# Linear attention and SwiGLU in one kernel: zero matmuls in the awaited bank, a group in halves, and a new order

## The chip, the core and the metric

The kernel runs on one core of a Trainium2 chip. The metric is device time of one execution in microseconds (us). A core has engines that run their own instruction streams side by side: TensorE (PE in the profile, its weight loads PEld), VectorE (DVE), ScalarE (ACT), GpSimd (POOL) and SyncE (SP), which here only issues transfers. Each works through its instructions in order and waits on semaphores for the others. Matmuls write to PSUM, of which this kernel uses eight banks; transfers between memory and SBUF run on 16 DMA engines.

## The reference

Four sequences of 768 tokens, 8 heads of 48: a linear attention with a decay of its own for each channel (RWKV-6), and behind it a feed-forward block over the 3072 rows of 384.

```python
for t in range(S):
    cur = np.einsum('bhd,bhe->bhde', u[None] * kt, vt)
    y[:, :, t] = np.einsum('bhd,bhde->bhe', rt, state + cur)
    state = wt[:, :, :, None] * state + np.einsum('bhd,bhe->bhde', kt, vt)
...
rms = np.sqrt(np.mean(x * x, axis=-1, keepdims=True) + 1e-06)
xn = x / rms * rms_g
g = xn @ w_gate
silu = g * (1.0 / (1.0 + np.exp(-g)))
return (silu * (xn @ w_val) @ w_out)
```

Inputs and output are float32; `w_gate` and `w_val` are 384x1536, `w_out` is 1536x384.

## The kernel before, in words

The 768 tokens are cut into six chunks of 128, so there are 24 tiles (n, j): chunk n of sequence j. Each tile passes through small steps, each a function of (n, j):

- Loads on SP's queue: `load_r`, `load_k`, `load_v`, `load_w` (L246 to L270). Each of r, k and v has eight buffers; the ninth load waits until the first tile's are read. For chunks 0 and 1 w comes in one load.
- Decay: `ln` (ACT, L383), `cs_mm` (PE, L391: running sums by a triangular matrix, 384 columns, and eight matmuls of one column for the totals), `exp_r` and `exp_k` (ACT), then `r_mul`, `w_tot` (DVE) and `k_mul` (DVE, or POOL for the tiles in `K_POOL`), which write the scaled r and k. From chunk 2 on `cs_add` (DVE) makes the second sum.
- Transposes of scaled r and k: for chunks 0 and 1 `rk_pe` (PE, L470, eight matmuls into one bank) and `rk_tr` (L476), which copies the bank of 128x1024 two-byte values to SBUF, on ScalarE; later chunks use a DMA transpose on SP's queue.
- Scores: `q_mm` (PE, L485) into an even and an odd bank; `q_mask_e` (DVE) masks the even one; the odd one is either masked on VectorE (`ODD_DVE`) or copied by ScalarE (`q_copy_o`) and masked on POOL (`q_mask_o`).
- Bonus of the current token: `bonus_mul` (POOL, two products), `bonus_sum` (DVE), `bonus_v` (POOL). `cast_v` (POOL or, for `CAST_ACT`, ACT) makes v two bytes wide.
- Output and state: `y_mm` (PE, L532), `x_add` (DVE), `st_mm` (PE), `st_new` (DVE).
- Norm: `x_sq` (ACT), `x_rstd` (ACT or POOL), `xn_mul` (ACT); then for chunks 0 to 3 `xn_pe` (PE) and `xn_out` (DVE, times the gain), for chunks 4 and 5 a DMA transpose `xn_tr` and `xn_gain` (POOL).

The feed-forward part works on six groups of four tiles, 512 columns. For each of twelve slices f of 128 hidden units there are `gate_mm` and `val_mm` (three matmuls of 512 columns each, L600), `silu` (ACT) and `h_mul` (DVE). A gate and val pair is called two units here. Then come four `o_mm` of twelve matmuls of 384 columns (L630), `o_out` and `out_dma`; the last tile's output is cut in two halves of 192. Groups are not chunks: `COL` (L193) puts tiles (1,0) and (1,1) in group 0 and (0,2) and (0,3) in group 1, so group 0 is (0,0), (0,1), (1,0), (1,1), and the feed-forward part starts when these four have passed the norm. What comes before is called the head.

Weights come on POOL's queue and are made two bytes wide on the way: `load_gv` g.h (L348; g 0 is slices 0 to 3, g 1 slices 4 to 11; h 0 gate, 1 val) and `load_wo`.

PSUM banks stand in three rings (L220): a and b of two banks each, for sums, gate and val, and q of four for the rest. `psum` (L223) gives a step the bank of its ring that came free first.

The order of all steps is written out in `ORDER` (L25), and the engines' streams follow from it, as `manual_schedule` adds waits but moves nothing. It was found by annealing against a planner's costs. `warm` steps (L372) are zero matmuls of 384 columns into a bank of ring q that nothing reads: 15 stand in the head, 6 behind the last output matmul. Two small matmuls for u and the gain stand ahead of all steps (L332 to L337).

Of the kernel before, what the change touches and what calls it, by code (L numbers as in the profile page):

```python
# [30 lines left out]
bonus_v.0.0 load_w.0.3 q_mask_o.0.0 q_mm.1.0 k_mul.0.1 q_mask_o.1.0 cast_v.0.0 r_mul.1.1 rk_pe.0.1 y_mm.0.0 k_mul.1.1
load_r.0.2 warm.16.0 rk_pe.1.1 x_add.0.0 w_tot.0.1 st_mm.0.0 load_v.0.1 bonus_mul.0.1 load_gv.0.0 q_mask_e.1.0
rk_tr.0.1 bonus_sum.0.1 warm.14.0 ln.0.3 st_new.0.0 x_sq.0.0 load_v.1.1 q_mm.0.1 x_rstd.0.0 q_mask_e.0.1 y_mm.1.0
x_add.1.0 rk_tr.1.1 cast_v.1.1 cast_v.0.1 load_w.0.2 bonus_sum.1.1 xn_mul.0.0 bonus_v.0.1 load_k.0.3 load_r.0.3
cs_mm.0.3 bonus_v.1.1 q_mask_o.0.1 w_tot.1.1 st_mm.0.1 y_mm.0.1 x_add.0.1 x_sq.1.0 exp_r.0.3 ln.0.2 q_mm.1.1
load_k.0.2 st_mm.1.1 q_mask_e.1.1 cs_mm.0.2 st_new.0.1 q_mask_o.1.1 xn_pe.0.0 y_mm.1.1 load_gv.0.1 xn_out.0.0
load_gv.1.0 x_sq.0.1 exp_k.0.3 load_v.0.2 x_rstd.1.0 load_v.0.3 x_rstd.0.1 k_mul.0.3 xn_mul.0.1 exp_r.0.2 x_add.1.1
xn_pe.0.1 xn_mul.1.0 xn_pe.1.0 bonus_mul.0.3 load_k.1.2 warm.15.0 warm.10.0 xn_out.0.1 x_sq.1.1 xn_out.1.0 x_rstd.1.1
xn_mul.1.1 warm.6.0 r_mul.0.3 w_tot.0.3 warm.18.0 st_mm.1.0 xn_pe.1.1 rk_pe.0.3 xn_out.1.1 r_mul.0.2 load_r.1.2
w_tot.0.2 exp_k.0.2 gate_mm.0.0 val_mm.0.0 gate_mm.0.3 silu.0.0 load_gv.1.1 silu.0.3 h_mul.0.0 gate_mm.0.1 val_mm.0.3  # L40
gate_mm.0.2 bonus_sum.0.3 k_mul.0.2 silu.0.1 val_mm.0.1 gate_mm.0.9 rk_tr.0.3 h_mul.0.3 silu.0.2 silu.0.9 load_v.1.2
q_mm.0.3 load_k.1.3 st_new.1.1 val_mm.0.2 gate_mm.0.8 bonus_mul.0.2 q_copy_o.0.3 h_mul.0.1 gate_mm.0.5 rk_pe.0.2
h_mul.0.2 silu.0.8 rk_tr.0.2 st_new.1.0 gate_mm.0.6 val_mm.0.9 q_mm.0.2 load_r.1.3 silu.0.5 h_mul.0.9 val_mm.0.8
cast_v.0.2 q_mask_e.0.3 h_mul.0.8 cs_mm.1.2 q_copy_o.0.2 q_mask_o.0.3 load_v.1.3 bonus_sum.0.2 load_w.2.0 silu.0.6
exp_k.1.2 cast_v.0.3 st_mm.0.2 st_mm.0.3 y_mm.0.3 q_mask_o.0.2 load_w.2.1 bonus_v.0.2 st_new.0.3 cs_mm.1.3 exp_r.1.2
load_w.2.2 q_mask_e.0.2 load_r.2.0 val_mm.0.6 bonus_v.0.3 exp_k.1.3 exp_r.1.3 r_mul.1.2 load_wo.1.0 y_mm.0.2 k_mul.1.2
w_tot.1.2 val_mm.0.5 gate_mm.0.4 rk_pe.1.2 silu.0.4 h_mul.0.6 val_mm.0.4 st_new.0.2 h_mul.0.5 load_wo.0.0 rk_tr.1.2
gate_mm.0.11 silu.0.11 x_add.0.3 r_mul.1.3 q_mm.1.2 x_sq.0.3 q_copy_o.1.2 load_w.2.3 bonus_mul.1.2 load_wo.2.0
w_tot.1.3 k_mul.1.3 bonus_sum.1.2 val_mm.0.7 cast_v.1.2 h_mul.0.4 cast_v.1.3 q_mask_o.1.2 rk_pe.1.3 q_mask_e.1.2
rk_tr.1.3 gate_mm.0.7 gate_mm.0.10 silu.0.7 y_mm.1.2 q_mm.1.3 x_add.0.2 val_mm.0.11 h_mul.0.7 val_mm.0.10 x_sq.0.2  # L50
q_copy_o.1.3 x_rstd.0.3 bonus_v.1.2 x_add.1.2 h_mul.0.11 st_mm.1.3 xn_mul.0.3 silu.0.10 x_rstd.0.2 load_r.2.1
h_mul.0.10 bonus_mul.1.3 q_mask_o.1.3 ln.2.0 xn_pe.0.3 xn_out.0.3 q_mask_e.1.3 o_mm.0.0 y_mm.1.3 cs_mm.2.0
bonus_sum.1.3 x_sq.1.2 x_rstd.1.2 ln.2.1 o_out.0.0 load_k.2.0 cs_add.2.0 xn_mul.0.2 xn_mul.1.2 load_r.2.2 ln.2.2
o_mm.0.2 st_new.1.3 load_r.2.3 exp_r.2.0 xn_pe.0.2 load_k.2.1 load_k.2.2 bonus_v.1.3 x_add.1.3 x_sq.1.3 ln.2.3
cs_mm.2.1 cs_add.2.1 x_rstd.1.3 exp_r.2.1 o_out.0.2 xn_mul.1.3 load_k.2.3 xn_pe.1.2 o_mm.0.1 w_tot.2.0 r_mul.2.0
r_mul.2.1 bonus_mul.2.0 cs_mm.2.3 w_tot.2.1 exp_k.2.0 k_mul.2.0 cs_mm.2.2 xn_out.1.2 exp_k.2.1 k_mul.2.1 xn_pe.1.3
out_dma.0.0 bonus_mul.2.2 cs_add.2.2 exp_k.2.2 cs_add.2.3 exp_r.2.3 xn_out.1.3 o_mm.0.3 rk_tr.2.0 xn_out.0.2 rk_tr.2.1
exp_r.2.2 w_tot.2.2 r_mul.2.2 st_mm.1.2 val_mm.1.4 r_mul.2.3 gate_mm.1.6 w_tot.2.3 exp_k.2.3 o_out.0.3 gate_mm.1.4
silu.1.6 bonus_mul.2.3 k_mul.2.2 k_mul.2.3 val_mm.1.6 h_mul.1.6 silu.1.4 h_mul.1.4 gate_mm.1.7 gate_mm.1.10 st_new.1.2
load_v.2.1 bonus_sum.2.0 val_mm.1.10 load_v.2.0 silu.1.10 silu.1.7 bonus_mul.2.1 val_mm.1.7 gate_mm.1.5 o_out.0.1  # L60
# [628 lines left out]
```

## Time and profile before

| | |
|---|---|
| three runs | 205.40, 206.16 (median), 279.91 us |
| profiled execution | 206.26 us |
| its span, first to last instruction | 204.5 us |
| first gate matmul starts | 30.89 us |
| last output matmul starts its twelve | 200.38 us |
| DMA | 32.41 MB, mean 158 GB/s |

In rows of the timeline the first number is the start, the second the length until the last of the group has ended; matmuls overlap, so the distance between starts tells their pace. In a bracket stands how long the engine was idle ahead of the row and what it waited for. In rows of groups the busy time comes first, then the mean length of one in ns, then idle time. The granted clock is a share of TensorE's full clock.

### The profile page before, as it was taken

To read this page: it belongs to the slowest core of one execution; us is meant where nothing else is said; L and a number is where in the kernel's file an instruction comes from. 1 tells how busy PE (TensorE), PEld (TensorE's weight loads), DVE (VectorE), ACT (ScalarE), POOL (GpSimd) and SP (SyncE) were. 2 spreads that over 40 slices of the span, in tenths; PEclk is the share of its full clock that TensorE was granted. 3 is DMA by queue.
4 is the path that set the end of the run, shared out by engine and by line. 5 is a ranking of instruction groups with operands and counts; after the bars stand their busy time and mean duration, and the time that the engine had idled before them with its cause. 6 is when DMAs were issued, how large, how long until landed. Compare 5 with 4: busy or idle time off the path is not lost.

```text
span 204.5 us, 4369 instructions
## 1 busy us (share of the span) xinstructions
PE 191.3 (94%) x1553; PEld 113.5 (55%) x1573; DVE 151.7 (74%) x298; ACT 144.4 (71%) x287; POOL 126.6 (62%) x186
## 2 busy tenths in 40 slices
...
GB/s 148 239 222 229 196 179 205 191 194 194 188 187 170 185 186 197 214 192 212 208 160 219 227 208 160 213 189 114 69 196 125 90 23 20 77 0 74 83 58 98
DMA packets 121566, 32.41 MB, mean 158 GB/s; under 512 B 116420, under 2 KB 120392, under 8 KB 121544
## 3 DMA queue, kind: packets, MB, share of 16 engines
...
q14 instruction: 10, 0.08, 0.1%
...
## 4 chain that ended last, share of the span: by engine, by line
PE 69%; DMA 12%; POOL 8%; DVE 3%; issue 3%; ACT 2%; POOLq 1%; SPq 0%; DVEq 0%; ACTq 0%
PE ps_bu L602 10%; PE ps_av L602 9%; PE ps_au L602 9%; PE ps_bv L602 9%; PE ps_qz L634 5%; DMA wv_sb<-in_moe_w_val_dram 5%; PE ps_qx L634 4%; PE ps_qu L634 3%; DMA wo_sb<-in_moe_w_out_dram 3%; PE ps_qv L634 3%; DMA vt<-in_v_dram 2%; POOL ruk L458 2%; DMA rkT<-rk 1%; POOL ruk L457 1%; DMA xnt<-xn 1%
## 5 line engine op out<-in xcount | busy, mean ns | idle before, releaser
L620 DVE TENSOR_TENSOR ht<-ps_bu,sg 128x512 bf16<-128x512 f32 x38 | 26.1, 686 | 16.9 <-PE ps_bu L602 12.8
L634 PEld LDWEIGHTS <-ht 128*128 128x128 bf16 x300 | 28.3, 98 | 17.2 <-issue 0.4
L602 PEld LDWEIGHTS <-wg_sb 128*128 128x128 bf16 x216 | 23.7, 114 | 22.7 <-issue 2.3
L236 ACT ACTIVATE sg<-ps_av 128x512 bf16<-128x512 f32 x38 | 22.7, 597 | 14.0 <-PE ps_av L602 11.9
L602 PEld LDWEIGHTS <-wv_sb 128*128 128x128 bf16 x216 | 22.4, 115 | 17.9 <-DMA wv_sb<-in_moe_w_val_dram 0.4
L602 PE MATMUL ps_av<-xnt,wg_sb 128*128 128x512 bf16 x111 | 30.5, 379 | 0.4 <-DVE xnt L588 0.2
L602 PE MATMUL ps_bu<-xnt,wv_sb 128*128 128x512 bf16 x103 | 30.2, 381 | 0.6
L457 POOL TENSOR_TENSOR ruk<-rt,kt 128x384 f32<-128x384 f32 x24 | 24.7, 1028 | 9.2 <-DMA rt<-in_r_dram 8.7
L620 DVE TENSOR_TENSOR ht<-ps_bv,sg 128x512 bf16<-128x512 f32 x34 | 23.3, 686 | 8.5 <-PE ps_bv L602 5.2
L602 PE MATMUL ps_au<-xnt,wg_sb 128*128 128x512 bf16 x97 | 27.0, 380 | 1.2 <-POOL xnt L593 0.8
L236 ACT ACTIVATE sg<-ps_au 128x512 bf16<-128x512 f32 x34 | 20.3, 597 | 10.4 <-PE ps_au L602 8.3
L602 PE MATMUL ps_bv<-xnt,wv_sb 128*128 128x512 bf16 x101 | 27.6, 381 | 0.0
L458 POOL TENSOR_TENSOR ruk<-ruk,u_bc 128x384 f32<-128x384 f32 x24 | 24.6, 1024 | 1.9
L467 POOL TENSOR_TENSOR ydiag<-vt,diag 128x384 f32<-128x384 f32 x24 | 19.8, 831 | 5.7 <-DVE diag L462 5.7
L234 ACT ACT_TABLE_LOAD x16 | 20.5, 1283 | 1.9 <-PEq L673 1.6
L510 POOL TENSOR_SCALAR_AFFINE_SELECT qts<-qts 128x512 bf16<-128x512 bf16 x20 | 12.6, 638 | 13.3 <-ACT qts L503 13.3
L634 PE MATMUL ps_qz<-wo_sb,ht 128*128 128x384 bf16 x96 | 17.1, 326 | 0.2 <-DMA wo_sb<-in_moe_w_out_dram 0.2
L563 ACT ACTIVATE xn<-xb,rstd 128x384 bf16<-128x384 f32 x24 | 14.3, 606 | 3.8 <-POOL rstd L559 3.6
L550 ACT ACTIVATE junk<-xb 128x384 bf16<-128x384 f32 x24 | 12.4, 518 | 6.0 <-DVE xb L545 5.5
L634 PE MATMUL ps_qx<-wo_sb,ht 128*128 128x384 bf16 (+1 forms) x84 | 13.8, 315 | 0.0
L462 DVE TENSOR_REDUCE diag<-ruk 128x8 f32<-128x384 f32 x24 | 12.8, 542 | 0.5 <-POOL ruk L458 0.5
L236 ACT ACTIVATE lw<-wt 128x384 bf16<-128x384 f32 (+1 forms) x20 | 11.4, 579 | 1.5 <-DMA wt<-in_w_dram 1.4
...
## 6 DMA issues: line engine op xcount, KB each, us to landing
...
wg_sb<-in_moe_w_gate_dram POOLq DMA_DIRECT2D x1, 768.0 KB, 10.4
```

Source lines behind the costliest of these rows:

```text
L234: nc.scalar.preload_act_table_set(table_name)
L236: return nc.scalar.activation(**kw).ins
L457: nc.gpsimd.tensor_tensor(out=ruk[n, j], in0=inp["r", n, j], in1=inp["k", n, j], op=ALU.mult)
L458: nc.gpsimd.tensor_tensor(out=ruk[n, j], in0=ruk[n, j], in1=u_bc, op=ALU.mult)
L462: nc.vector.tensor_reduce(out=diag[n, j].rearrange("p h o -> p (h o)"), in_=ruk[n, j], axis=mybir.AxisListType.X, op=ALU.add)
L467: nc.gpsimd.tensor_tensor(out=ydiag[n, j], in0=inp["v", n, j], in1=diag[n, j].to_broadcast([128, H, D]), op=ALU.mult)
L510: nc.gpsimd.affine_select(out=qts[n, j][:, 1], in_=qts[n, j][:, 1], compare_op=ALU.is_gt, fill=0.0, base=0, pattern=[[0, NP], [1, 128]], c ...
L550: nc.scalar.activation(out=junk, in_=xb[n, j], func=AF.Square, accum_out=rstd[n, j][:, 0:1])
L563: nc.scalar.activation(out=xn, in_=xb[n, j], func=AF.Copy, scale=rstd[n, j][:, 1:2])
L602: nc.tensor.matmul(ps, lhsT=units(ws, c, f), rhs=xnt[n].rearrange("p (c x) -> p c x", c=KC)[:, c, :], start=(c == 0), stop=(c == KC - 1))
L620: nc.vector.tensor_tensor(out=ht[n][:, f, :], in0=bank.pop(("v", n, f)), in1=bank.pop(("sg", n, f)), op=ALU.mult)
L634: nc.tensor.matmul(ps[:, cols], lhsT=ht[n][:, f, b * L:(b + 1) * L], rhs=wo_sb[:, f, cols], start=(f == 0), stop=(f == FC - 1))
```

## The change

1. `warm` steps are gone. A step in `ORDER` may carry a number (`q_mm.1.1:7`): so many zero matmuls are put into the bank that the step's first tile takes, ahead of the step's own. There are 50 at 17 steps: 48 up to `val_mm.0.0`, with which the feed-forward part now starts (four at that step itself), and one each at `gate_mm.0.6` and `gate_mm.0.11`.
2. The matmuls for u and the gain become steps (`u_mm`, `u_out`, `g_mm`, `g_out`); u stays at the start, the gain moves behind `y_mm.0.1`.
3. Group 1 is (0,2), (1,2), (0,3), (1,3), and its units work on half of the columns and two slices: six matmuls of 256 columns in place of three of 512. Units 0 to 5 belong to the first two tiles, 6 to 11 to the others.
4. Choices of engine change for many tiles: seven of the eight `rk_tr` copies go to VectorE (`RK_DVE`), more odd masks to VectorE, more `k_mul` to POOL, more `cast_v` to ScalarE.
5. The whole of `ORDER` is new. In the head all loads of chunks 0 and 1 are issued ahead of any other, r before w; `load_gv` comes in the order small val, small gate, large gate, large val.

```diff
-warm.20.0 load_w.0.0 warm.2.0 warm.8.0 warm.9.0 warm.11.0 load_k.0.0 load_k.1.0 ln.0.0 cs_mm.0.0 load_r.0.0 exp_k.0.0
-cs_mm.1.0 exp_r.0.0 exp_r.1.0 r_mul.0.0 w_tot.0.0 k_mul.0.0 warm.3.0 warm.0.0 rk_pe.0.0 exp_k.1.0 load_w.0.1 k_mul.1.0
...
+load_r.0.0 load_w.0.0 u_mm.0.0 ln.0.0 load_v.0.0 load_k.0.0 cs_mm.0.0:2 load_r.1.0 load_w.0.1 u_out.0.0 load_k.1.0
+load_k.0.1 load_w.0.3 load_v.0.1 exp_r.0.0 exp_k.0.0 r_mul.0.0 cast_v.0.0 load_r.0.1 bonus_mul.0.0 load_k.1.1
+bonus_sum.0.0 bonus_v.0.0 k_mul.0.0 cs_mm.1.0 load_r.1.1 load_v.1.1 load_v.1.0 load_w.0.2 rk_pe.0.0:2 rk_tr.0.0
...
-    CAST_ACT = sel("00 10 20 21 40 41 42")
+    CAST_ACT = sel("00 01 02 03 20 21 30 31 33 40 43 53")
-    K_POOL = sel("02 03 20 21 23 31 33 41 51 52 53")
+    K_POOL = sel("02 10 20 21 22 23 30 31 32 33 40 42 43 50 51 53")
-    RK_DVE = sel("")
-    ODD_DVE = sel("00 01 10 11")
-    RSTD_ACT = sel("00 01 02 11 32 42")
+    RK_DVE = sel("00 02 03 10 11 12 13")
+    ODD_DVE = sel("00 02 10 11 13 20 23 40 43 52")
+    RSTD_ACT = sel("00 10 11 13 20 32 33")
-    COL = {(0, 2): (1, 0), (0, 3): (1, 1), (1, 0): (0, 2), (1, 1): (0, 3)}
+    COL = {(0, 2): (1, 0), (1, 2): (1, 1), (0, 3): (1, 2), (1, 3): (1, 3), (1, 0): (0, 2), (1, 1): (0, 3)}
+    HALF = (1,)
...
+        if ahead[at[0]]:
+            spare = psP.tile([128, 512], FP32, name="ps_" + ring + "uvxz"[k])
+            for _ in range(ahead[at[0]]):
+                nc.tensor.matmul(spare[:, 0:DM].rearrange("p (a x) -> p a x", a=3), lhsT=zero, rhs=bc_mid(zero, 3),
+                                 start=True, stop=True)
+            ahead[at[0]] = 0
...
+    def half_of_group(f):
+        h, p = f // (FC // 2), f % (FC // 2)
+        return slice(h * TS // 2, (h + 1) * TS // 2), 2 * p
+
     def fc_mm(ps, ws, n, f):
-        for c in range(KC):
-            nc.tensor.matmul(ps, lhsT=units(ws, c, f), rhs=xnt[n].rearrange("p (c x) -> p c x", c=KC)[:, c, :],
-                             start=(c == 0), stop=(c == KC - 1))
+        x = xnt[n].rearrange("p (c x) -> p c x", c=KC)
+        if n not in HALF:
+            for c in range(KC):
+                nc.tensor.matmul(ps, lhsT=units(ws, c, f), rhs=x[:, c, :], start=(c == 0), stop=(c == KC - 1))
+            return
+        cols, f = half_of_group(f)
+        for i in range(2):
+            for c in range(KC):
+                nc.tensor.matmul(ps[:, i * TS // 2:(i + 1) * TS // 2], lhsT=units(ws, c, f + i), rhs=x[:, c, cols],
+                                 start=(i == 0 and c == 0), stop=(i == 1 and c == KC - 1))
...
+        if n in HALF:
+            cols, f = half_of_group(f)
+            nc.vector.tensor_tensor(out=ht[n][:, f:f + 2, cols], in0=v.rearrange("p (i x) -> p i x", i=2),
+                                    in1=sg.rearrange("p (i x) -> p i x", i=2), op=ALU.mult)
```

The order of TensorE's steps up to the first units of group 0, afterwards:

```
u_mm.0.0 cs_mm.0.0:2 cs_mm.1.0 rk_pe.0.0:2 st_mm.0.0 q_mm.0.0:4 cs_mm.0.1 rk_pe.1.0 q_mm.1.0:2 cs_mm.1.1 rk_pe.0.1:2
y_mm.0.0 st_mm.0.1:4 cs_mm.0.3:3 q_mm.0.1:1 y_mm.1.0 rk_pe.1.1:1 q_mm.1.1:7 y_mm.0.1:8 g_mm.0.0 y_mm.1.1 xn_pe.1.0:2
xn_pe.0.0 cs_mm.0.2 st_mm.1.1:3 st_mm.1.0 xn_pe.0.1 rk_pe.0.3:3 xn_pe.1.1 val_mm.0.0:4 gate_mm.0.3 val_mm.0.3
q_mm.0.3 gate_mm.0.2 gate_mm.0.0 rk_pe.0.2 val_mm.0.2 gate_mm.0.5 gate_mm.0.1 val_mm.0.1 gate_mm.0.6:1 gate_mm.0.11:1
q_mm.0.2 gate_mm.0.8 val_mm.0.6
```

And of POOL's, up to the large val weights: `bonus_mul.0.0 bonus_v.0.0 k_mul.1.0 bonus_mul.1.0 bonus_mul.0.1 load_gv.0.1 bonus_v.0.1 cast_v.1.0 bonus_v.1.0 cast_v.1.1 bonus_mul.1.1 load_gv.0.0 q_mask_o.0.1 bonus_v.1.1 load_gv.1.0 x_rstd.0.1 load_gv.1.1`.

More of the change, by code (lines that the diff above doesn't have):

```diff
@@ L31 @@
[L31 to L60, printed above, removed]
```

248 lines of the change are left out of this document (137 added, 111 removed).

## The prediction

> **What bounds the kernel now.** I read the page's busy shares first, then busy time by stretch, then TensorE's own waits.
>
> ```profile
> PE 191.3 (94%) x1553; PEld 113.5 (55%) x1573; DVE 151.7 (74%) x298; ACT 144.4 (71%) x287; POOL 126.6 (62%) x186
> ```
>
> ```profile
> 10.15:30.75 20.60, 16.96 (x200) 11.53 (x199) 16.81 (x36) 17.29 (x38) 16.70 (x22) 0.83 1.10 206
> 30.89:63.22 32.33, 31.91 (x284) 19.22 (x288) 26.64 (x55) 28.20 (x54) 21.29 (x32) 1.00 1.01 193
> 63.22:91.73 28.51, 28.35 (x246) 16.95 (x247) 26.39 (x54) 24.74 (x49) 22.03 (x32) 1.00 0.98 190
> 15.00:17.50 2.50, 0.46 (x12) 0.30 (x11) 2.17 (x4) 2.44 (x5) 2.50 (x3) 1.00 1.08 231
> 18.70:25.90 7.20, 6.73 (x71) 4.60 (x72) 6.30 (x14) 6.05 (x15) 5.21 (x9) 0.53 1.15 216
> 30.89:201.40 170.51, 167.04 (x1317) 98.15 (x1337) 131.09 (x250) 123.66 (x245) 103.84 (x148) 1.00 0.73 152
> ```
>
> The columns are the stretch, its length, busy time of PE, PEld, DVE, ACT and POOL, then the granted clock and DMA. From the first gate matmul (30.89) to the last output matmul (201.40) TensorE is busy 167.04 of 170.51 us at full clock: this part is TensorE's throughput, and 3.5 us of it is waiting. Before 30.89 it is a head in which the work of four tiles passes from engine to engine; VectorE is busy 16.81 of 20.60 us there. So a change can win only a shorter head and those 3.5 us. TensorE's waits:
>
> ```profile
> PE ps_qz L492 <- ACT rkT L483: 2.0, 1, 2.0
> PE ps_au L602 <- POOL xnt L593: 0.8, 1, 0.8
> PE ps_av L411 <- ACT ek L236: 0.7, 1, 0.7
> PE ps_qx L492 <- DMA rkT<-rk: 0.4, 1, 0.4
> PE ps_au L411 <- ACT lw L236: 0.2, 1, 0.2
> ```
>
> Only the first is in the head; the other four sum to 2.1 us. The profiled execution took 206.26 us, 1.76 more than its span of 204.5 and 0.10 more than the median; the sum is made against 206.26.
>
> **Head: its start.**
>
> ```profile
> 4.16 1.64 PE L333 MATMUL ps_qu<-u_bc,ones_row 1*128 1x384 f32 x2 [4.16 <-POOL ones_row L329]
> 6.88 0.53 PE L374 MATMUL ps_qv<-zero 128*128 128x384 bf16 x1
> 7.20 0.53 PE L374 MATMUL ps_qx<-zero 128*128 128x384 bf16 x1
> 7.52 0.85 PE L396 MATMUL ps_au<-lw,mw 128*128 128x384 bf16 x2
> 8.16 0.40 PE L400 MATMUL ps_au<-mw,lw 128*128 128x1 bf16 x8
> 8.42 0.80 PE L403 MATMUL ps_bu<-lw,mw 128*128 128x384 bf16 x2
> ```
>
> ```profile
> 4.34 0.84 ACT L236 ACTIVATE lw<-wt 128x768 bf16<-128x768 f32 x1 [1.42 <-DMA wt<-in_w_dram]
> 9.26 0.47 ACT L236 ACTIVATE ps_bu<-ps_bu 128x384 f32<-128x384 f32 x1 [4.07 <-PE ps_bu L403]
> 9.65 0.47 ACT L236 ACTIVATE ps_au<-ps_au 128x388 f32<-128x388 f32 x1
> ```
>
> ```profile
> 10.15 0.55 DVE L445 TENSOR_TENSOR rk<-rt,ps_au 128x384 bf16<-128x384 f32 x1 [3.69 <-ACT ps_au L236]
> 30.27 0.56 DVE L588 TENSOR_TENSOR xnt<-ps_qv,gT 128x384 bf16<-128x384 bf16 x1 [0.62 <-PE ps_qv L578]
> ```
>
> Now the first cs_mm waits behind the gain matmul and five zero matmuls, although its logarithm is done at 5.18. Afterwards only the u matmul (to 5.80) and two zero matmuls of 0.32 stand ahead: it starts at 6.44. The logarithm is no later, since r is now loaded ahead of w, some 0.9 us, and 4.34 + 0.9 + 0.84 = 6.1. Its r sum takes 8.42 - 7.52 = 0.90 and is done at 7.34; exp_r is now first on ACT, 0.24 later (as 9.02 to 9.26 now), and r_mul 0.50 behind it (9.65 to 10.15): 8.08 in place of 10.15, **-2.1 us**.
>
> **Head: VectorE's work.** Up to the last xn_out VectorE runs the same steps in both, but afterwards three rkT copies (RK_DVE: 00, 10, 11) that ScalarE makes now, and one odd mask fewer. No row has VectorE copying rkT's 1024 two-byte values out of PSUM; the nearest:
>
> ```profile
> L334 DVE COPY u_bc<-ps_qu x1: 558/558/558, 5.8 to 5.8; 128x384 f32<-128x384 f32 x1
> L499 DVE TENSOR_TENSOR qts<-ps_qu,mask_lt 128x512 bf16<-128x512 f32 x9 | 6.1, 682 | 0.6 <-PE ps_qx L494 0.6
> ```
>
> Steps overlap by 0.08 (a row of 0.47 and the next 0.39 later, above), so a mask costs 0.6. A copy of 384 values takes 0.56, so it cannot be less. From 384 to 512 values a VectorE row grows by 0.13, or 1.05 ns a value; 512 more make 0.68 + 0.54 = 1.22 the other end. I take 0.90, half way: the 384-value rows show no gain for two-byte data (xnt 0.56, f32 0.55), but they are not copies. After overlap three copies add 2.46 (1.4 to 3.4). VectorE's waiting in the head (20.60 - 16.81 = 3.8 us) I leave as it is: the new order removes the wait on rkT, but puts each step behind others. Head: -2.1 + 2.46 - 0.6 = **-0.25** (-1.3 to +0.7); the first feed-forward matmul at 30.6. The Trainium skill ("VectorE: DVE Perf Modes", the perf-mode tier table) gives a copy out of PSUM up to twice the plain rate; that would make the copy 0.68 as an estimate and the head -0.9, and no run here shows it yet.
>
> **Zero matmuls.** Fifty instead of 21, 48 of them up to the first feed-forward step. Each takes 0.16 us at full clock. They sit behind the bank's release and ahead of the step, so they fill a wait; where the operand is there earlier than the planner thought, each delays its step by 0.16. The largest packs (7 before q_mm.1.1, 8 before y_mm.0.1) stand where I find q_mm.1.1 waiting for a copy that waits on VectorE for some 1.2 us; cost nothing, up to 1 us if that cover is gone. The two ahead of gate_mm.0.6 and 0.11 stand in a stretch without waits: **+0.3**. The six behind the last output matmul go; there the store sets the end: 0.
>
> ```profile
> 202.45 0.32 PE L374 MATMUL ps_qv<-zero 128*128 128x384 bf16 x1
> ```
>
> **Second group in halves.** Its 72 matmuls of 512 columns become 144 of 256. A price stands in the last output tile, which is already cut:
>
> ```profile
> 195.49 1.15 PE L634 MATMUL ps_qu<-wo_sb,ht 128*128 128x192 bf16 x12
> 196.48 2.11 PE L634 MATMUL ps_qz<-wo_sb,ht 128*128 128x384 bf16 x12
> 198.43 2.11 PE L634 MATMUL ps_qv<-wo_sb,ht 128*128 128x384 bf16 x12
> ```
>
> Twelve of 192 columns start 0.99 us apart, twelve of 384 1.95: two halves cost 0.03 us per twelve more, so weight loads stay hidden; 72 pairs cost **+0.2**. silu and h_mul keep their 512 columns. The halves let group 1 start with (0,2) and (1,2) alone, but TensorE does not wait there now (63.22 is reached without an idle row), so nothing is gained directly.
>
> **Weights.** On POOL's queue load_gv order changes.
>
> ```profile
> 24.13 0.81 POOL L351 DMA_DIRECT2D wv_sb<-in_moe_w_val_dram  x1
> 24.93 0.77 POOL L351 DMA_DIRECT2D wg_sb<-in_moe_w_gate_dram  x1
> 29.57 0.85 POOL L351 DMA_DIRECT2D wv_sb<-in_moe_w_val_dram  x1
> ```
>
> ```profile
> wv_sb<-in_moe_w_val_dram POOLq DMA_DIRECT2D x1, 768.0 KB, 10.0
> ```
>
> ```profile
> q0 software_dynamic: 407, 0.41, 64.4%
> ```
>
> ```profile
> q1 hardware_dynamic: 1879, 0.36, 44.5%
> ```
>
> ```profile
> 45.91 0.61 PE L474 MATMUL ps_qz<-ident,rk 128*128 128x128 bf16 x8
> 46.36 0.81 PE L602 MATMUL ps_bu<-xnt,wv_sb 128*128 128x512 bf16 x3
> 47.01 0.81 PE L602 MATMUL ps_av<-xnt,wg_sb 128*128 128x512 bf16 x3
> ```
>
> The two queue rows (packets, MB, share of the 16 DMA engines) are POOL's weights from 24.9 to 29.5 and SP's loads from 35.0 to 39.5. Now the last three (384 + 768 + 768 KB) go out from 24.13 and land by 29.57 + 10.0 = 39.6. Afterwards the small val load goes out near 16.8; ahead of the small gate load POOL has four bonus_mul (two products of 1.0 each), three bonus_v (0.8), a k_mul (1.0), two casts (0.5) and a load (0.9), 13.3 us from 7.1, and some 2.5 us of waits: near 23. The large ones follow near 25.6 and 27.4. The same 1920 KB in the same 15.4 us land by 38.4. The first use of the large val part, val_mm.0.6, comes after twelve units of three matmuls (0.65, 46.36 to 47.01), a rk_pe (0.45, 45.91 to 46.36), two q_mm (0.3) and two zero matmuls, 9.2 us behind 30.6, at 39.8: covered by 1.4 us, cost 0. All 24 loads of r, k and v of the first two chunks now stand ahead of it on SP too, so this cover is what can fail (below).
>
> **Waits that go.**
>
> ```profile
> 178.00 0.81 PE L602 MATMUL ps_au<-xnt,wg_sb 128*128 128x512 bf16 x2 [0.83 <-POOL xnt L593]
> ```
>
> The 0.8 on xnt stands ahead of the last group: between its last y_mm and its first gate_mm TensorE has four o_mm now (1.95 each, above), 7.8 us; afterwards seven units and three o_mm, 10.4 us. **-0.8**. Of the others (0.7, 0.4, 0.2) the new order keeps the same chain of log, sum and exp between o_mm steps; I take a third, **-0.4**, between 0 and -1.3.
>
> **Sum:** 206.26 - 0.25 + 0.3 + 0.2 - 0.8 - 0.4 = **205.3 us**. Its own range, from the copy's ends and the waits, is 203.3 to 206.9.
>
> **Rivals.** *VectorE becomes the bound.* In 30.89 to 63.22 it is busy 26.64 of 32.33; afterwards this stage has four more rkT copies and two odd masks, less one o_out and one xn_out. At 1.22 a copy that is 26.64 + 4.6 + 1.2 - 1.0 = 31.4; the next stage shows that VectorE keeps 2.1 us idle (28.51 - 26.39), so the stage would take 33.5, +1.2, and the head +0.7 in place of -0.25: 207.5. For it: no two-byte VectorE row is faster; against: ScalarE, which loses these copies, was busy 28.20 there.
>
> *The clock does not follow.* TensorE was busy 0.46 of 2.50 us from 15.00, and from 18.70 to 25.90 it had 0.53 of the clock. If zeros that wait for a bank come too late to keep it, or the early part (two zeros, not five, ahead of cs_mm) leaves it at half up to 15 rather than 12, cs_mm.0.1 and rk_pe.1.0 (0.8 + 0.45 at full clock) cost that much again: +1.2, 206.5. The Trainium skill ("TensorE: Matmul & The Clock Gate", Part 1) has the clock fall only after an idle window of about 3.4 us; here the longest wait ahead of the fall was 2.0 us in a stretch with some matmuls, so the trace does not agree, and by that rule the packs would hardly be needed.
>
> *Weights come late; slower.* With SP's loads queued without a break, the weights may move at the rate of the quoted queue row alone (0.41 MB in 24.9 to 29.5, 0.09 MB/us) in place of 1.97 MB in 15.4 us (0.13). Then the large gate part lands at 37.8, against 35.3 for gate_mm.0.5, and the large val part at 46.5 against 42.3: 2.5 + 4.2 = +6.7, 212.0. It decides (over 210.4) from about 0.1 MB/us down. Against it: SP's loads moved beside the weights in before as well, up to 39.5 (the q1 row).
>
> *Head closes up; faster.* If the order also takes 2 us of VectorE's 3.8 us of waiting, copies cost 0.68, and the remaining waits go: 205.3 - 2.0 - 0.65 - 0.9 = 201.8.
>
> **How the numbers follow.** The forecast 0.46, VectorE bound 0.18, clock 0.11, weights late 0.12 (a quarter of it short of 2%), head closes up 0.13. A difference of 2%, 4.1 us, is about what a measurement of this kernel can tell from none: faster, under 202.1, takes most of the last case and the forecast's edge, 0.14; slower, over 210.4, 0.11; same 0.75. The range runs from 201.3 to 209.0, which leaves out the worse weights cases and the best heads.
>
> **What would show it.** Right: r_mul near 8.1; first feed-forward matmul within 29.3 to 31.4; rkT copies on DVE between 0.56 and 1.22; TensorE idle before the last group gone; halves starting 0.11 us apart; clock full from 12 on. Wrong: TensorE waiting on wg_sb or wv_sb after 34; VectorE idle under 2 us in group 0's stage with TensorE waiting on ht or rkT; a new wait where group 1's second half needs (1,3), which is transposed only after group 1's first units.

## The result, and the profile after

The kernel after takes 206.40 us (median of 20 executions, 205.23 to 207.39), the kernel before 205.39 us (median of 20). The ratio is 1.0054 with a 95% interval of 1.0036 to 1.0072: 1.1 us slower, far less than 2%, yet clear of zero, where the sum had a gain of 0.96 us on before's profiled execution (206.26 to 205.3). (The ratios leave out executions more than 1.5% above the fastest of their kernel: here one of before, 279.91 us, and below it comes to five of twelve in two experiments of set 3, where it is said.) The profiled execution of after took 206.26 us with a span of 204.5, by chance the same two numbers as that of before. This matters below: before's profiled execution lay 0.87 us above its median of twenty, after's 0.14 below.

The page of the kernel after, busy shares and the granted clock in 40 slices:

```profile
PE 193.3 (94%) x1657; PEld 120.9 (59%) x1674; DVE 157.8 (77%) x307; ACT 134.8 (66%) x278; POOL 124.4 (61%) x178
...
PEclk9999999999999999999999999999999999999999
```

The granted clock on the page is full throughout, where before had 0.53 in 18.7 to 25.9. The first matmuls still run at half pace, as they did before: two sums of 384 columns take 0.64 us at 8.08 and 0.34 at 12.64. Its stretches: the head from the first r_mul to the end of the last xn_out, the stages of groups 0 and 1, and the feed-forward part.

```profile
8.17:31.04 22.87, 21.73 (x249) 13.61 (x247) 18.59 (x40) 15.72 (x37) 17.97 (x22) 1.00 1.10 212
31.19:64.33 33.14, 32.61 (x283) 19.15 (x288) 29.71 (x59) 24.70 (x51) 20.80 (x30) 1.00 1.02 192
64.33:93.26 28.93, 28.93 (x322) 24.64 (x319) 27.03 (x56) 22.63 (x49) 20.79 (x28) 1.00 1.04 189
31.19:201.10 169.91, 167.52 (x1393) 105.75 (x1410) 135.06 (x256) 116.31 (x239) 101.96 (x141) 1.00 0.75 152
```

The head starts 2 us earlier (8.17 against 10.15) and is 2 us longer, VectorE's busy time in it having grown to 18.59 us; the feed-forward part takes 169.91 us. The prediction's 170.51 for before ends at 201.40, ahead of the end of that kernel's last row (200.38 + 1.15 = 201.53), so the fairer pair runs from the first unit to the start of the last twelve output matmuls: 169.49 us before, 168.76 after, 0.73 less. TensorE's waits after:

```profile
PE ps_qu L496 <- DMA rkT<-rk: 0.9, 1, 0.9
PE ps_qx L496 <- DVE rkT L485: 0.5, 1, 0.5
PE ps_av L613 <- ACT sg L247: 0.2, 1, 0.2
PE ps_qx L656 <- DVE ht L642: 0.2, 1, 0.2
```

The wait on ScalarE's rkT (2.0) and that on xnt (0.8) are gone. The second row is the only one left in the head, apart from 4.2 us ahead of the very first matmul, which before has too. Outside the head 1.27 us remain, where before had 2.23: the prediction's four, and 0.16 on wo_sb. (Its list also left out 0.57 on xn and three waits of 0.2 in the head.) A wait on a DMA transpose at q_mm.4.0 has grown from 0.4 to 0.9.

Timeline rows of TensorE (L236 are the zeros), first at the end of the head, then at the two packs in group 0, then in the halved group:

```profile
28.96 0.65 PE L236 MATMUL ps_qv<-zero 128*128 128x384 bf16 x3
29.67 0.61 PE L478 MATMUL ps_qv<-ident,rk 128*128 128x128 bf16 x8
30.11 0.33 PE L582 MATMUL ps_qz<-ident,xn 128*128 128x128 bf16 x3
30.28 0.81 PE L236 MATMUL ps_bv<-zero 128*128 128x384 bf16 x4
31.19 0.81 PE L613 MATMUL ps_bv<-xnt,wv_sb 128*128 128x512 bf16 x2
...
37.92 0.33 PE L236 MATMUL ps_av<-zero 128*128 128x384 bf16 x1
38.30 0.81 PE L613 MATMUL ps_av<-xnt,wg_sb 128*128 128x512 bf16 x3
38.94 0.33 PE L236 MATMUL ps_au<-zero 128*128 128x384 bf16 x1
39.33 0.81 PE L613 MATMUL ps_au<-xnt,wg_sb 128*128 128x512 bf16 x3
...
64.33 0.82 PE L618 MATMUL ps_bv<-xnt,wv_sb 128*128 128x256 bf16 x6
64.99 0.82 PE L618 MATMUL ps_av<-xnt,wg_sb 128*128 128x256 bf16 x6
65.64 0.82 PE L618 MATMUL ps_bu<-xnt,wv_sb 128*128 128x256 bf16 x6
```

The gate matmul behind a single zero starts 0.38 us (38.30 - 37.92) and 0.39 us after it, not 0.16. No other engine is waited for in between. The step writes the bank that the zero writes, so my theory was that TensorE waits for its own zero to be out of the array; sets 2 and 4 below bear that out. I call the 0.22 us beyond 0.16 the hand-over. A halved unit takes 0.655 us, a whole one 0.648.

When the groups' first units and the last twelve output matmuls start, in us, from the same kind of rows in the profiled execution of each kernel (the last four are experiments below):

| kernel | 0 | 1 | 2 | 3 | 4 | 5 | last twelve |
|---|---|---|---|---|---|---|---|
| before | 30.89 | 63.22 | 91.73 | 122.05 | 150.39 | 178.00 | 200.38 |
| after | 31.19 | 64.33 | 93.26 | 122.35 | 151.21 | 175.62 | 199.95 |
| after, no packs in group 0 | 30.51 | 62.90 | 91.83 | 120.48 | 149.03 | 173.43 | 197.77 |
| after, head delayed | 34.27 | 67.42 | 96.34 | 124.99 | 153.16 | 177.56 | 201.89 |
| before, no zeros at the end | 30.87 | 63.79 | 92.30 | 121.76 | 149.75 | 176.72 | 199.09 |
| before, no first five zeros | 29.21 | 62.23 | 90.74 | 120.67 | 148.67 | 177.61 | 199.99 |

### The profile page after: what moved, and what is told of

It is laid out like the page before. It is cut to its first block, busy times and chain, and to the rows that moved or that the text cites. A ratio compares the mean times of both kernels' runs of the same rounds, so it can differ in the third digit from the quotient of the medians.

```text
span 204.5 us, 4563 instructions
## 1 busy us (share of the span) xinstructions
PE 193.3 (94%) x1657; PEld 120.9 (59%) x1674; DVE 157.8 (77%) x307; ACT 134.8 (66%) x278; POOL 124.4 (61%) x178
## 4 chain that ended last, share of the span: by engine, by line
PE 59%; DMA 4%; ACT 3%; DVE 2%; POOL 1%; SPq 1%; issue 1%; ACTq 0%; DVEq 0%; POOLq 0%
PE ps_qx L656 6%; PE ps_au L613 6%; PE ps_av L613 6%; PE ps_qv L656 6%; PE ps_bu L613 6%; PE ps_bv L613 5%; PE ps_qu L656 5%; PE ps_qz L656 4%; DMA rkT<-rk 2%; PE ps_au L618 2%; PE ps_bu L618 2%; DMA vt<-in_v_dram 2%; PE ps_av L618 2%; PE ps_bv L618 2%; ACT L245 1%
## 5 line engine op out<-in xcount | busy, mean ns | idle before, releaser
L642 DVE TENSOR_TENSOR ht<-ps_bv,sg 128x512 bf16<-128x512 f32 x29 | 19.9, 685 | 13.9 <-PE ps_bv L613 13.0
L613 PEld LDWEIGHTS <-wg_sb 128*128 128x128 bf16 x180 | 19.2, 114 | 16.7 <-issue 1.6
L613 PE MATMUL ps_av<-xnt,wg_sb 128*128 128x512 bf16 x88 | 25.0, 381 | 0.6 <-ACT sg L247 0.2
L642 DVE TENSOR_TENSOR ht<-ps_bu,sg 128x512 bf16<-128x512 f32 x31 | 21.2, 684 | 5.4 <-PE ps_bu L613 3.3
L613 PE MATMUL ps_bu<-xnt,wv_sb 128*128 128x512 bf16 x86 | 24.8, 379 | 0.4
L613 PE MATMUL ps_au<-xnt,wg_sb 128*128 128x512 bf16 x87 | 23.6, 380 | 0.1
L613 PE MATMUL ps_bv<-xnt,wv_sb 128*128 128x512 bf16 x82 | 23.2, 380 | 0.3
L455 POOL TENSOR_TENSOR rk<-kt,ek 128x384 bf16<-128x384 f32 x16 | 15.9, 1001 | 9.9 <-ACT ek L247 5.7
L656 PE MATMUL ps_qx<-wo_sb,ht 128*128 128x384 bf16 x96 | 17.1, 326 | 0.2 <-DVE ht L642 0.2
L656 PE MATMUL ps_qv<-wo_sb,ht 128*128 128x384 bf16 (+1 forms) x84 | 13.8, 314 | 0.0
```

The lines of the kernel that those rows point to most:

```text
L455: eng.tensor_tensor(out=rk[:, n % 2, j, 1, :, 0:D], in0=inp["k", n, j], in1=bank["cs_k", n, j][:, 0:DM].rearrange("p (h d) -> p h d", h=H) ...
L613: nc.tensor.matmul(ps, lhsT=units(ws, c, f), rhs=x[:, c, :], start=(c == 0), stop=(c == KC - 1))
L642: nc.vector.tensor_tensor(out=ht[n][:, f, :], in0=v, in1=sg, op=ALU.mult)
L656: nc.tensor.matmul(ps[:, cols], lhsT=ht[n][:, f, b * L:(b + 1) * L], rhs=wo_sb[:, f, cols], start=(f == 0), stop=(f == FC - 1))
```

## The experiments

Sixteen kernels in four sets; each set ran on one chip together with the kernel before, and each ratio is to before on that chip. Before's own median was 204.7 to 206.4 us there, so only ratios are compared between sets; a difference of two ratios carries about 0.003 to 0.005.

### Set 1: what the zeros cost and bring

Three theories stood at the start: the zeros delay their own steps (A); the new order costs and the zeros pay (B); and before's profiled execution was a poor one.

*After, without any zero* (all `:m` gone from `ORDER`):

```diff
-... cs_mm.0.0:2 ... q_mm.1.1:7 ... y_mm.0.1:8 ... val_mm.0.0:4 ... gate_mm.0.6:1 gate_mm.0.11:1
+... cs_mm.0.0 ... q_mm.1.1 ... y_mm.0.1 ... val_mm.0.0 ... gate_mm.0.6 gate_mm.0.11
```

> The kernel after, without any of its 50 zero matmuls; order and banks stay. Theory A (zeros delay): each pack costs its zeros and a hand-over of some 0.2 us wherever the step's operands are there already; the two packs in group 0 took 0.38 and 0.39 us in the trace after, and the one ahead of the first feed-forward matmul and rk_pe.0.3's some 0.6 together, so this runs 1 to 2 us below the kernel after: 204.4 to 205.4 us, ratio to before 0.995 to 1.000, at a clock that stays above 0.98. Theory B (the new order costs, the zeros pay): without them the granted clock falls as it did in before's profile (0.53 in 18.7 to 25.9, which is 3.4 us of full-speed work), and this takes 208 to 210 us, ratio 1.013 to 1.022, with a clock near 0.97.

Measured: 1.0014 (0.9987 to 1.0042). The mean clock fell, to 0.975 in the profiled execution and 0.987 in the median one, as B says, but the time did not rise with it. The stretch row shows the clock:

```profile
22.00:31.00 9.00, 6.68 (x70) 5.47 (x71) 6.50 (x15) 7.53 (x21) 6.39 (x10) 0.51 1.05 184
```

Nine microseconds at half clock, and the first feed-forward unit came at 31.63, 0.44 us behind after's. B's 1.013 is excluded; A's range ends at 1.000, inside the interval, but its clock above 0.98 held in only eight executions of twelve.

*After, without the two packs in group 0:*

```diff
-gate_mm.0.6:1 gate_mm.0.11:1
+gate_mm.0.6 gate_mm.0.11
```

> The kernel after without the two zero matmuls ahead of gate_mm.0.6 and gate_mm.0.11; the 48 of the head stay. Theory A (a hand-over behind each pack, 0.38 us for a pack of one where TensorE has no wait): 0.7 to 0.8 us less than after, 205.6 to 205.7 us, ratio 1.001 to 1.002. Theory B (zeros fill time that is waited anyway, the order costs): 0 to 0.3 less, 206.1 to 206.4, ratio 1.0035 to 1.005.

Measured: 0.9997 (0.9972 to 1.0022), 1.2 us (give or take 0.6) below after for two zero matmuls. The sign and at least the size of A; B's 1.0035 lies outside the interval. The two units now follow one another at 0.65 us:

```profile
37.24 0.81 PE L613 MATMUL ps_av<-xnt,wg_sb 128*128 128x512 bf16 x3
37.89 0.81 PE L613 MATMUL ps_au<-xnt,wg_sb 128*128 128x512 bf16 x3
```

*Before, without any zero:*

```diff
-warm.20.0 load_w.0.0 warm.2.0 warm.8.0 warm.9.0 warm.11.0 load_k.0.0 ... warm.3.0 warm.0.0 rk_pe.0.0 ...
+load_w.0.0 load_k.0.0 ... rk_pe.0.0 ...
```

> The kernel before without any of its 21 zero matmuls (five of them stand ahead of the first running sum, ten more in the head, six at the end). Theory A: the clock is lost and won by a few tenths of a microsecond of chance, the ten in the head do little for it; the first running sum starts about 1.0 us earlier: 204.4 to 205.6, ratio 0.995 to 1.001. Theory B: zeros hold the clock; without them 2 us or more are lost at half clock: above 207, ratio above 1.01, clock at or under 0.975.

Measured: 0.9921 (0.9889 to 0.9954): 1.6 us faster than before, with the same clock (0.983 in the median execution). A, and more than it asked for.

*Before, without the six zeros at the end:*

```diff
-o_mm.5.1 o_mm.5.4 out_dma.5.2 warm.5.0 out_dma.5.3 o_out.5.0 out_dma.5.0 warm.12.0 warm.1.0 o_out.5.1 warm.17.0
+o_mm.5.1 o_mm.5.4 out_dma.5.2 out_dma.5.3 o_out.5.0 out_dma.5.0 o_out.5.1
```

> The kernel before without the six zero matmuls behind the last output matmul; the head is untouched, so the clocks of its runs tell how often before's head loses the clock. Both theories: the time stays, ratio 0.998 to 1.002. If the profiled execution of before (0.983, 206.26 us against a median of 205.39) was one of its poorer ones, most runs here show a clock above 0.985 and times near 205.4; if that loss is the rule, they show 0.983 and the 0.9 us between that execution and the median have another cause.

Measured: 0.9987 (0.9965 to 1.0009), so they cost nothing that can be seen. Its twelve executions had clocks of 0.982 to 0.992, and the 32 of before beside them 0.983 (17 of them), 0.992 (12) and 1.00 (3): losing the clock for some microseconds is before's rule, not an accident. But the waits of this execution, whose steps up to the last output matmul are before's, are not those that the prediction had read:

```profile
PE ps_qz L633 <- DMA wo_sb<-in_moe_w_out_dram: 0.5, 1, 0.5
PE ps_au L601 <- POOL xnt L592: 0.3, 1, 0.3
PE ps_au L601 <- ACT sg L235: 0.2, 1, 0.2
...
PE ps_au L410 <- DVE rk L450: 0.2, 1, 0.2
```

The wait on xnt is 0.3 in place of 0.8, that of 0.7 on ek is not there, one on wo_sb has grown to 0.5, and all waits behind the head sum to 1.25 us in place of 2.23. What the prediction had read belonged to one execution. But this execution too lies above the median of its twelve (204.92 against 204.43), so these waits alone do not tell a typical execution from a long one.

### Set 2: price of a pack, of the halves, of the copies

*After with eight more packs of one, in group 2:*

```diff
-gate_mm.2.10 ... gate_mm.2.9 ... gate_mm.2.11 ... gate_mm.2.4 ... gate_mm.2.7 ... gate_mm.2.3 ... gate_mm.2.5 ... gate_mm.2.1
+gate_mm.2.10:1 ... gate_mm.2.9:1 ... gate_mm.2.11:1 ... gate_mm.2.4:1 ... gate_mm.2.7:1 ... gate_mm.2.3:1 ... gate_mm.2.5:1 ... gate_mm.2.1:1
```

> The kernel after with one zero matmul more, in the awaited bank, ahead of each of eight gate steps of group 2, where TensorE has no wait: ten such packs of one in place of two. Theory A (a pack of one takes the 0.38 us of the trace after, zero plus hand-over): 8 x 0.38 = 3.0 us over the kernel after, ratio to before 1.020. Rival B (only the zero's own 0.16 us counts, the rest would have been waited anyway): 1.3 us, ratio 1.012.

*The same ten single zeros in banks of their own:*

```diff
-gate_mm.0.6:1 gate_mm.0.11:1 ... gate_mm.2.10:1 ...
+warm.108.0 gate_mm.0.6 warm.109.0 gate_mm.0.11 ... warm.100.0 gate_mm.2.10 ...
```

> The same ten single zero matmuls, but each in a bank of its own from ring q, as the kernel before had them; the one for gate_mm.2.3 stands seven steps earlier since no bank is free there. Theory A (it is the shared bank that costs: the step must see the zero done before it may write): 0.16 us each, so the two of group 0 get 0.45 cheaper and the eight cost 1.3: 0.85 us over the kernel after, ratio 1.009 to 1.010, and 2.2 us below the run with ten in awaited banks. Rival B (a bank of its own is no cheaper): no difference between the two runs, ratio 1.012 or more for both.

Measured: 1.0102 (1.0068 to 1.0137) and 1.0047 (1.0020 to 1.0073). The rows in group 2 show A's price at each place, 0.38 us in the awaited bank (from the zero's start at 96.07 to the step's at 96.45) and 0.16 in an own one (97.77 to 97.93). But the whole time grew by 1.0 us (give or take 0.8) and by nothing. So A is right at the place and wrong in the sum: group 2's stage was 2.6 us longer, and by the first unit of group 5 the profiled execution had 0.2 of that back. The median had more back. Set 4 asks this again where nothing follows that could give time back.

*After with groups 1 to 5 in halves:*

```diff
-    HALF = (1,)
+    HALF = (1, 2, 3, 4, 5)
```

> The kernel after with groups 1 to 5 in halves in place of group 1 alone: 288 matmuls of 512 columns become 576 of 256. The prediction's term is 0.2 us a group, the trace's pace (0.655 against 0.648 us a unit) gives 0.15: 0.6 to 0.8 us more than after, ratio 1.008 to 1.0095. Rival: group 1 takes 28.93 us from its first unit to the next group's in three kernels with halves and 28.51 in three without; if that 0.42 is the halves', 1.7 us more, ratio 1.0135.

Measured: 1.0109 (1.0074 to 1.0144): 1.1 us (give or take 0.8) for four more groups, 0.28 each. It holds the prediction's 0.2 and does not exclude the rival's 0.42.

*After with all eight rkT copies on ScalarE:*

```diff
-    RK_DVE = sel("00 02 03 10 11 12 13")
+    RK_DVE = sel("")
```

> The kernel after with all eight rkT copies on ScalarE (RK_DVE empty), as before; the order stays. If VectorE's copies are what eats the head's early start (the prediction's +2.46 us, at 0.69 a copy in the trace 1.8), the head gets 1 us or more shorter: ratio 0.996 to 1.001. If ScalarE's copy (1.01 us) and ScalarE's queue are the worse place, the time rises by 0.5 us or more: ratio above 1.008. In between, the choice of engine does not matter here.

Measured: 1.0214 (1.0166 to 1.0263), the first feed-forward unit at 34.18. VectorE is the better place; in this order the copies cannot go back:

```profile
PE ps_qu L496 <- DMA rkT<-rk: 2.7, 1, 2.7
PE ps_qz L496 <- ACT rkT L487: 1.8, 3, 0.9
```

### Set 3: the zeros of the head apart

*Before without its first five zeros:*

```diff
-warm.20.0 load_w.0.0 warm.2.0 warm.8.0 warm.9.0 warm.11.0 load_k.0.0
+load_w.0.0 load_k.0.0
```

> The kernel before without its first five zero matmuls, which stand ahead of the first running sum; the other 16 stay. Without any zeros the first sum started at 5.95 in place of 7.52, r_mul at 8.55 in place of 10.15, and the ratio was 0.992. Theory A (that start is all of it): 0.991 to 0.994 here too. Rival B (the ten zeros inside the head, each ahead of a step that is ready, cost the larger part): 0.996 to 1.000.

Measured: 0.9981 (0.9953 to 1.0009), in B's range, but B's reason is not shown: the run without any zeros, which lacks the ten as well, had its first feed-forward unit later than this one (30.10 against 29.21). And the mechanism of A is there in full: the first r_mul at 8.55, and the first feed-forward unit 1.7 us earlier (29.21). It is given back later (the table's last row: by the last twelve nothing remains but 0.4 us against before, and it stands 0.9 behind the run without the end's zeros). Where, these rows say:

```profile
154.65 0.23 PE L491 MATMUL ps_qz<-rkT 48*128 48x128 bf16 x1 [0.71 <-DMA rkT<-rk]
177.61 0.81 PE L601 MATMUL ps_au<-xnt,wg_sb 128*128 128x512 bf16 x3 [1.43 <-POOL xnt L592]
```

TensorE came earlier to chunk 5, and waited for its transposes.

*Part 1 of the change alone: before with its head's zeros in the awaited bank* (with the change's code for packs, and none at the end):

```diff
-warm.20.0 ... warm.11.0 ... cs_mm.0.0 ... warm.3.0 warm.0.0 rk_pe.0.0 ... warm.19.0 cs_mm.0.1 ... warm.13.0 ... rk_pe.1.0
+cs_mm.0.0:5 ... rk_pe.0.0:2 ... cs_mm.0.1:1 ... rk_pe.1.0:1
-... warm.16.0 rk_pe.1.1 ... warm.14.0 ... q_mm.0.1 ... warm.15.0 warm.10.0 ... warm.6.0 ... warm.18.0 st_mm.1.0
+... rk_pe.1.1:1 ... q_mm.0.1:1 ... st_mm.1.0:4
```

> Part 1 of the change alone: the kernel before with its 15 zeros of the head put into the bank of the next TensorE step that takes one (packs of 5, 2, 1, 1, 1, 1 and 4) in place of banks of their own; the six at the end are left out, which alone gave 0.9987. Theory A (a pack in the awaited bank adds 0.22 us of hand-over where TensorE is the late one): some of seven packs, 0.3 to 1.5 us, ratio 1.000 to 1.006. Rival B (inside the head TensorE waits for others anyhow, so the hand-over is covered; banks freed from ring q may even help): 0.996 to 0.999.

Measured: 1.0013 (0.9985 to 1.0042), inside A's range, with an interval that reaches into B's. Against the run without the end's zeros it is 0.5 us (give or take 0.7) slower: not told apart from nothing.

*After without the packs of group 0 and without the last four packs of the head:*

```diff
-xn_pe.1.0:2 ... st_mm.1.1:3 ... rk_pe.0.3:3 ... val_mm.0.0:4 ... gate_mm.0.6:1 gate_mm.0.11:1
+xn_pe.1.0 ... st_mm.1.1 ... rk_pe.0.3 ... val_mm.0.0 ... gate_mm.0.6 gate_mm.0.11
```

> The kernel after without the two packs in group 0 and without the last four packs of the head (xn_pe.1.0, st_mm.1.1, rk_pe.0.3, val_mm.0.0: 12 zeros); the other 36 zeros stay. Theory A (the late packs hold up the last transpose: xn was ready at 29.5, its transpose ran at 30.1): the first feed-forward unit 0.5 to 0.8 us earlier than with them, ratio 0.996 to 0.998. Rival B (the chain over VectorE and ScalarE sets the head, and late packs fill its waits): 0.999 to 1.001, like the run without the two packs in group 0 alone (0.9997).

Measured: 1.0025 (0.9986 to 1.0064), from seven executions of twelve; the median of all twelve, 208.30 us, is 1.009 of before's 206.38. A fell, as far as one trace of each can tell: the first unit started at 30.72, no earlier than with the packs (30.51 in the run without the two of group 0), and TensorE now showed waits where the packs had stood:

```profile
28.66 0.34 PE L582 MATMUL ps_qz<-ident,xn 128*128 128x128 bf16 x3 [0.69 <-ACT xn L567]
29.23 0.62 PE L478 MATMUL ps_qv<-ident,rk 128*128 128x128 bf16 x8 [0.23 <-DVE rk L449]
```

So zeros at the head's end did fill waits. Behind the head this trace lost more: from the first unit to the last twelve it took 171.4 us, against 167.3 for the same steps in the run without the two packs of group 0 alone.

*Before without zeros, r ahead of w, exp_r first:*

```diff
-load_w.0.0 load_k.0.0 load_k.1.0 ln.0.0 cs_mm.0.0 load_r.0.0 exp_k.0.0 cs_mm.1.0 exp_r.0.0
+load_r.0.0 load_w.0.0 load_k.0.0 load_k.1.0 ln.0.0 cs_mm.0.0 exp_r.0.0 exp_k.0.0 cs_mm.1.0
```

> The kernel before without zeros (0.992), and with the first tile's r loaded ahead of its w and exp_r.0.0 ahead of exp_k.0.0, as the kernel after starts. If the first r_mul sets the head, it comes 0.4 us earlier and so does all that follows: 0.989 to 0.991. If VectorE's and ScalarE's chain behind it has slack there, nothing changes: 0.991 to 0.993.

Measured: 0.9900 (0.9861 to 0.9939), the lowest of all, but from seven executions of twelve; the median of all twelve, 205.28 us, is 0.995 of before's 206.38. r_mul came 1.0 us earlier than without the swap (7.56 against 8.55), the first feed-forward unit only 0.06 (30.04 against 30.10); the swap's own worth is not shown.

### Set 4: what was still open

*After with one zero ahead of each of the twelve gate steps of the last group, in the awaited bank:*

```diff
-gate_mm.5.1 val_mm.5.1 gate_mm.5.0 ...
+gate_mm.5.1:1 val_mm.5.1 gate_mm.5.0:1 ...
```

> The kernel after with one zero matmul in the awaited bank ahead of each of the twelve gate steps of the last group, which waits for nothing and behind which only the output follows. Theory A (0.38 us a pack: the zero's 0.16 and 0.22 of hand-over): 4.6 us over the kernel after, ratio to before 1.027 to 1.029. Rival B (a pack costs the zero's 0.16 and no more in the whole time): 1.9 us, ratio 1.014 to 1.016.

*The same twelve in banks of their own:*

```diff
-gate_mm.5.1 val_mm.5.1 gate_mm.5.0 ...
+warm.100.0 gate_mm.5.1 val_mm.5.1 warm.101.0 gate_mm.5.0 ...
```

> The same twelve zeros in banks of their own (two of them stand a step or two earlier, where a bank is free). Theory A: 0.16 us each, 1.9 us over the kernel after, ratio 1.014 to 1.016, 2.7 us below the run with packs. Rival B: no difference between the two runs. Rival C (a zero in a bank of its own is free): ratio 1.005 to 1.007.

Measured: 1.0267 (1.0224 to 1.0311) and 1.0180 (1.0138 to 1.0223). Over after that is 4.4 us (give or take 1.0), 0.37 a pack, and 2.6 us (give or take 0.9), 0.22 a zero. The rows, first with packs, then with own banks:

```profile
187.11 0.33 PE L236 MATMUL ps_au<-zero 128*128 128x384 bf16 x1
187.49 0.81 PE L613 MATMUL ps_au<-xnt,wg_sb 128*128 128x512 bf16 x2
188.14 0.33 PE L236 MATMUL ps_av<-zero 128*128 128x384 bf16 x1
```

```profile
187.09 0.33 PE L365 MATMUL ps_qv<-zero 128*128 128x384 bf16 x1
187.25 0.81 PE L614 MATMUL ps_av<-xnt,wg_sb 128*128 128x512 bf16 x3
```

The last group's stretch shows the same: 24.33 us after, 28.51 with packs, 26.55 with own banks. Theory A holds: 0.38 us a pack where TensorE is the late one. The zero's 0.16 and a hand-over of 0.22. The Trainium skill ("TensorE: Matmul & The Clock Gate", Single matmul latency) gives a lone matmul a fixed 0.17 us or so beside its columns; by that a 384-column zero lasts some 0.33 us as an estimate, and the trace, at 0.38, agrees but for 0.05.

*After with the head 1.95 us later:*

```diff
-val_mm.0.0:4
+val_mm.0.0:16
```

> The kernel after with twelve zeros more ahead of the first feed-forward unit: the head ends 1.95 us later. Theory A (from there on TensorE's work sets the end): all of it is seen, ratio 1.014 to 1.016. Rival C (later waits on transposes and inputs give part back: 0.9 us on rkT ahead of q_mm.4.0 in the trace after): 0.9 to 1.2 us are seen, ratio 1.0095 to 1.0115.

Measured: 1.0102 (1.0066 to 1.0138), 1.0 us (give or take 0.8) over after: C. In the profiled execution the first unit came 3.1 us later than after's (1.1 of that is not the zeros'; the head shows a wait of 0.5 on a logarithm more), the last twelve 1.9 later. Of the 1.2 us between, stages 2 and 3 gave back 0.4 and 0.7, the latter as the wait ahead of q_mm.4.0 shrank:

```profile
PE ps_qu L496 <- DMA rkT<-rk: 0.2, 1, 0.2
```

*Before without zeros, r first, and the last group in halves* (with the change's code for halves):

```diff
+    HALF = (5,)
-gate_mm.5.5 silu.5.5 val_mm.5.5 h_mul.5.5 gate_mm.5.8 val_mm.5.8 ...
+gate_mm.5.0 silu.5.0 val_mm.5.0 h_mul.5.0 gate_mm.5.1 val_mm.5.1 ...
```

> The kernel before without zeros and with r first (0.990), and with the last group in halves, its twelve units renumbered so that the first six need the first two tiles alone: part 3 of the change, put where TensorE waits for xnt (0.3 to 1.4 us in the traces of before's order). If that wait stands in most executions: 0.5 to 1.2 us less, less 0.15 for the halves, ratio 0.985 to 0.988. If it only takes up what came early elsewhere, nothing or the price of the halves: 0.990 to 0.992.

Measured: 0.9925 (0.9890 to 0.9960). TensorE no longer waited for xnt ahead of the last group, and the time is not shorter than without the halves (0.9900). But the kernel that this one is built on has no such wait in its trace either. Its last output matmuls ahead of the group start at 174.12 and need 1.95 us to the next start, so TensorE stood 0.13 us there:

```profile
174.12 2.11 PE L632 MATMUL ps_qv<-wo_sb,ht 128*128 128x384 bf16 x12
176.20 0.81 PE L600 MATMUL ps_au<-xnt,wg_sb 128*128 128x512 bf16 x3
```

So there was next to nothing to take off, and what the halves are worth where that wait stands was not tried; a gain of a few tenths is not excluded, as the intervals overlap.

## Why the prediction was wrong, point by point

Two steps failed above all. The waits counted as gains were those of one execution, and the zeros ahead of two units of group 0 were priced without their hand-over. In their place the runs show a feed-forward part whose waits change from execution to execution, and two packs without which the time is before's again (0.9997).

- *Head, its start, -2.1.* Right: r_mul at 8.17, forecast 8.08. That such a gain reaches the head's end was seen once (before without its first five zeros: r_mul 1.6 us earlier, first unit 1.7) and once not (with r first: 1.0 and 0.06).
- *Head, VectorE's work.* The three copies took 0.69 us each, not 0.90; the rule of the Trainium skill quoted in the prediction ("VectorE: DVE Perf Modes", the tier table, estimate 0.68) fits, and half way between the two ends did not. VectorE's busy time still grew by 1.8 us (18.59 - 16.81), as forecast (1.86): what the copies saved, a k_mul of 1.03 us and other steps took.
- *"VectorE's waiting ... I leave as it is".* It was 22.87 - 18.59 = 4.3 us, not 3.8. With that the head's net is +0.30 us in this execution (first unit at 31.19; forecast 30.6). In the run without group 0's packs, whose head is the same, it was 30.51: that spread is as large as the term.
- *A head's microsecond is a microsecond of the end.* Never written down, but the sum used it, and it failed. A head 1.7 us shorter gave 0.4 us (give or take 0.6); one delayed by 1.95 us cost 1.0. Behind the head stand waits of TensorE on transposes of later chunks, which grew in the trace that came early and shrank in the one that came late. How much they vary: in six traces of before's order (before, and its variants with no change in the feed-forward part) the same steps from the first unit to the last twelve took 167.9 to 170.8 us.
- *Zeros in the feed-forward part, +0.3.* Mis-sized: 0.77 us in the rows, 0.37 a pack in the whole time (set 4), and 1.2 us (give or take 0.6) by taking the two away. The hand-over was missing from the sum.
- *Zeros in the head, nothing; up to 1 us if the cover is gone.* Right so far as can be measured: all fifty gone gave 0.8 us (give or take 0.7) less than after, the two of group 0 alone 1.2. What the zeros' delays cost in the head and what the clock that they keep brings were not told apart.
- *Halves, +0.2.* Right: 0.655 against 0.648 a unit is 0.15, and 0.28 by the run with five groups.
- *Weights, 0.* Right: no wait on them.
- *Waits that go, -0.8 and -0.4.* **The step that turned the sign.** They were read in one execution that lay 0.87 us above before's median; in a second one of the same order the wait on xnt was 0.3 and that on ek absent, and over the six traces of before's order TensorE stood 0.1 to 1.4 us ahead of the last group. Without these two terms the sum gives 206.5, no gain at all; with them it gives 205.3, the time that before had already (205.39). That just these waits make up the 0.87 us is argued, not shown. The feed-forward part of the two profiled executions shortened as summed (-0.73 against +0.3 + 0.2 - 0.8 - 0.4 = -0.7), but in part by luck: the zeros took 0.77 there in place of 0.3, so some 1.65 us went in place of 1.2, and the waits in the lists fell by only 1.0.
- *Behind the last output matmul, 0.* From the start of the last twelve to the end of the span there are 4.55 us, before 4.12: +0.43. That is more than the chance of one trace: before and its six variants have 4.11 to 4.17, after and its ten 4.15 to 4.81. The zeros are not the cause (0.9987 without them). The last copy starts 1.19 us behind the last twelve in both, but it is VectorE's now and 0.04 longer, and from its end to the end of the span, in which its store runs, there are 3.0 us in place of 2.6; why the store takes longer was not tried. The two rows, before and after:

```profile
201.57 0.32 ACT L643 COPY ob<-ps_qx 128x192 f32<-128x192 f32 x1 [0.47 <-PE ps_qx L634]
201.14 0.36 DVE L663 COPY ob<-ps_qu 128x192 f32<-128x192 f32 x1 [0.38 <-PE ps_qu L656]
```

So against before's profiled execution the sum missed by 0.55 in the head, next to nothing in the feed-forward part as a whole and 0.43 at the end, and against the median by 0.87 more. (The upper end of its own range, 206.9, does not come out of its terms, which give 206.7.) Against the medians, the two packs of group 0 are as large as the whole loss, and new order, choices of engine and early head together bring nothing that can be measured.

Of the rivals, none came: the clock followed, VectorE's copies cost 0.69, no weight was late. The clock rival priced the fall at 1.2 us, and the runs do not settle that price. Before's executions at 0.983 and 0.992, on the four chips, differ by 0.0 to 0.5 us in the mean, and the twelve at full clock lie 0.2 to 1.7 below the first, about 1.0 (give or take 0.4) over all four. On the other hand before without zeros was the faster one at the lower clock, and after, at 0.997 to 1.00 in all its twenty executions, shows no such gain. In before's head VectorE was busy 16.81 of 20.60 us, which fits a head that TensorE's pace does not set; no run held VectorE's work apart to show it.
